# One segment's attention by halves of queries, masked keys by DMA, and a re-valued order

## The chip, the cores and the metric

The kernel runs on one core of one Trainium2 chip. The time is the device time of one execution in microseconds (us). A profiled execution gives a span (first to last instruction) and, beside it, its own device time, which is a little longer.

## What is computed

Two layers of the same pair of blocks run over a sequence of 2048 rows of 512 features: memory-augmented attention (32 heads of 16 features, four segments of 512 rows), then a gated feed-forward part of width 1792. The essential lines:

```python
# attention, per segment s of 512 rows; M and z carry over from segment to segment
logits = einsum('bhqd,bhkd->bhqk', qs, ks) * scale + mask     # causal inside the segment
a_dot = einsum('bhqk,bhkd->bhqd', softmax(logits), vs)
a_mem = einsum('bhld,bhde->bhle', phi(qs), M) / (einsum('bhld,bhd->bhl', phi(qs), z) + 1e-6)
o = g * a_mem + (1 - g) * a_dot
M, z = M + phi(ks)^T vs, z + sum(phi(ks))
# network, twice over
x = x + attention(layernorm(x));   x = x + (gelu(n @ w_gate) * (n @ w_up)) @ w_down   with n = layernorm(x)
```

Segment 0 has no memory, so its attention is the causal part alone. All inputs and the output are bf16.

## The kernel before

**Numbering.** `k` counts segments over both layers, 0 to 7; `Att(k)` and `Ffn(k)` (L610, L1019) are the attention and the feed-forward part of one of them. Attention of segment k+4 needs the output of `Ffn(k)`, and attention of k needs the memory of k-1. So the feed-forward work of one segment can stand beside the attention of the next.

**An order written ahead of time.** No loop nest runs on the chip. The function `order` (L286) holds a small simulation with one clock per engine (`Clocks`, `Engine`), a list of pieces of TensorE work (`Item`) and lists of jobs for VectorE, ScalarE, GpSimd and the SP queue. It walks forward in planned time, picks the next piece by due times and slacks, and emits the instruction there and then. Each engine's instructions are thus a fixed sequence, and semaphores make one wait for another. The due times come from the table `POLICY` of some 45 values: `gate_step`, `early`, `hold`, `cap` and so on. A change of any value may reorder the whole program, on each engine. Jobs carry a slack: `URGENT`, `SOON` or `NORMAL`, smaller first. When TensorE has nothing ready, it runs a filler product on the tile `warm`.

**Attention in rounds.** A segment's scores are 36 rounds (`STEPS`), nine for each block `b` of 128 columns (eight heads: four of parity 0, four of parity 1). A round is 256 columns of scores for four heads, in four row tiles of TensorE (L939). Rounds are issued in pairs into PSUM; ScalarE takes each pair in two exponentials of 128x1024 (L1399) into two of the ten slots of `pt`. The triangles are cut by GpSimd (L1346, L1351) or VectorE (L1356). A block's nine rounds are four of parity 0 (`FULL`), one shared by both parities (`PAIRED`, the diagonal pieces), and four of parity 1. The odd heads need a copy of k with the even heads' rows set to zero, and the shared round one that mixes the two: the masked k, `kx`, made by two instructions per block on VectorE, GpSimd (L417) or ScalarE (L422), whichever the planner picks. `kx` of segments 1 and up alternates between two buffers.

**From scores to the output of a block.** `flush_item` (L943) multiplies the exponentials with v (four column tiles, 40 products) into one PSUM bank for a block and a parity. VectorE turns it (`byq`, L972), inverts the sums (L976), scales (L980) and turns back (`aT`, L987). `flush_item` frees the slots of `pt` that it has used. After all four blocks, `wo` (four tiles of 128 rows, 4 products each) gives the attention output.

**From there to the feed-forward part.** The `wo` tile is added to x (L1028). VectorE takes the row's moments (`bn_stats` L514, `bn_aggr` L522). When all four tiles are in, GpSimd computes the inverse root for the four at once (L527, L532); VectorE scales four tiles (`xn`, L544), TensorE turns them (L586; for the keys in `BY_PE`, else a DMA transpose on SP does it), with `FILL` = 2 filler products on `warm` ahead of each (L584), and they are copied out into `xnT`. Then come 14 gate tiles, 14 up tiles (4 products each) and 4 down tiles of 14 products. The gate waits for all of `xnT`, and in segment 0 also for the memory update, since the gate's buffer `gel_sb` holds v of segment 0 until then.

**SP's queue.** SP issues the weights, the DMA transposes and the shared v (`vz`, L701) in one sequence. The pieces of `w_down` go out at fixed planned times from 94 us on, since q, k and `kx` of segment 0 lie in their place.

Of the kernel before, what the change touches and what calls it, by code (L numbers as in the profile page):

```python
# [12 lines left out]
ALU = mybir.AluOpType  # L13
# [18 lines left out]
VALUES = TPS * VW + 16  # L32
SCALE = DH ** -0.5
# [11 lines left out]
PAIRED = [(ki, P * ki, C, C * ki) for ki in range(TPS)]  # L45


def round_of(t):

    b, i = divmod(t, ROUNDS)  # L50
    if i == SHARED:
        return b, (0, 1), PAIRED, None
    par = int(i > SHARED)
    return b, (par,), FULL[i - par * (SHARED + 1)], DIAG[i - par * (SHARED + 1)]


BY_PE = {("xnTf", 0), ("xnTf", 1), ("xnTf", NK - 1)}
BANKS = 8
# [3 lines left out]
URGENT, SOON, NORMAL = -4.0, -1.5, 0.0  # L62
XN_BUFS = 4
BUFS = 6
FILL = 2
# [4 lines left out]
    flush_wait=60.178, piece_slack=2.474, kb_slack=40.846, mem_slack=-55.59, margin=2.052, qk_due=-2.997, e_q=-1.628,  # L70
    e_k=2.444, exp_slack=-52.211, e_slack=213.844, phi_slack=26.757, gelu_slack=17.711, act_evict=-7.207,
    first_evict=15.014, gate_step=70.271, up_due=-0.803, up_step=0.121, down_due=2.855, down_step=15.464,
    upd_due=-0.036, kb_act=30.625, vz_slack=-37.946, x_dve=-2.928, v0_due=-11.201, x1_at=-44.439, x2_at=17.127,
    x3_at=25.097, x3_load=11.502, direct=4, gelu_tiles=7, look=4.219, lag=0.576, wv_at=-5.253, xn_pool=39.635,
    kb_pool=0.131, cut_pool=-3.745, at_pool=5.073, pe_turns=0, gate_due=2.262, shun=0.829, col_gap=3.113, hold=3,
    early=122.612, starve=0.322, near=-0.26, cap=2, soon=21.81, columns=0)
# [15 lines left out]
class Engine:  # L92
# [24 lines left out]
    def serve(self, now):  # L117
# [9 lines left out]
        job = min((j for j in jobs if j[0] + self.LATENCY <= start + 0.03), key=lambda j: j[0] + j[1] + (  # L127
# [123 lines left out]
class Item:  # L251


    def __init__(self, due, ready, ops, done, kind, ps, after="start"):
        self.after = after
        self.due = due if callable(due) else lambda: due
        self.ready, self.ops, self.done, self.kind, self.ps = ready, ops, done, kind, ps
        self.posted = 0.0
# [27 lines left out]
def order(pol, nc, cst, seg, wrk, psp, A_x, A_wq, A_wk, A_wv, A_wo, A_beta, B_x, B_w_gate, B_w_up, B_w_down, out):  # L286
# [87 lines left out]
    nc.vector.reduce_sum(out=masks[:, 1:2], in_=bd[:, 16:P:32], axis=mybir.AxisListType.X)  # L374

    tmp_e2 = cst.tile([P, H], F32, name="tmp_e2")
# [34 lines left out]
    def masked_copies(ready, slack, kx, kf, told):  # L411
# [4 lines left out]
        def vector(which, eng):  # L416
            return lambda: eng.tensor_scalar(out=kx[:, :, C * which:C * which + P], in0=kf, scalar1=masks[:, which:which + 1],  # L417
                                             scalar2=None, op0=ALU.mult)
# [6 lines left out]
        ck.dve.post(ready, slack, (Port(0.35), vector(0, nc.vector), None),  # L425
                    (Port(0.35), vector(1, nc.vector), told), taken=taken)
        ck.pool.post(ready, slack + pol.kb_pool, (Port(1.57, True), vector(0, nc.gpsimd), None),
# [50 lines left out]
    def soon(name, n=KT, part=1.0):  # L478

        t = ck.pe - 0.1 - ck.back  # L480
# [20 lines left out]
    class Norm:  # L501
        def __init__(self, key, tt0, tag, slack, free):
            self.key, self.tt0, self.tag, self.slack, self.free = key, tt0, tag, slack, free
            self.mv, self.n, self.left = None, 0, TPS
# [3 lines left out]

        def stats(self, j, ready):
            def emit():  # L510
                if self.mv is None:
                    self.mv = self.small("mv", 2)
# [3 lines left out]
            def told(t):  # L516
                self.n += 1
                if self.n == TPS:
                    self.scales(t)

            ck.dve.post(ready, self.slack, (0.66, emit, None),
                        (0.17, lambda: nc.vector.bn_aggr(out=self.mv[:, j, :], in_=self.st6[:]), told))  # L522

        def scales(self, ready):
            def first():
                self.ve = wrk.tile([P, TPS, 1], F32, tag="lnve", name="ve")
                nc.gpsimd.tensor_scalar(out=self.ve[:], in0=self.mv[:, :, 1:2], scalar1=EPS_LN, scalar2=None,  # L527
                                        op0=ALU.add)

            def second():  # L530
                self.rs = self.small("rs", 1)
                nc.gpsimd.tensor_tensor(out=self.rs[:], in0=self.ve[:], in1=mhalf[:], op=ALU.pow)  # L532

            ck.pool.post(ready, URGENT, (0.25, first, None),
                         (1.05, second, lambda t: ck.when(self.free, lambda: self.start(max(t, ck.pe)))))

        def start(self, ready):
            self.xnT = seg.tile([P, KT, L], BF16, tag=self.tag, bufs=1, name="xnT")
            for j in range(TPS):
                xn_slots.take(lambda n, j=j: bufs.take(lambda i: self.row(j, n, i, max(ready, ck.pe))))  # L540

        def normed(self, j, i, eng=nc.vector):
            xn = buffer(i, "xn")
            eng.tensor_scalar(out=xn[:], in0=x_sb[:, self.tt0 + j, :], scalar1=self.mv[:, j, 0:1],  # L544
# [3 lines left out]
        def row(self, j, n, i, ready):  # L548
# [13 lines left out]
            def told(t):  # L562
                if self.by_pe():
                    items.append(self.turn_item(j, xn, t, landed))
                else:
                    turn_later(t, self.slack, lambda: self.xnT[:, :, j * P:(j + 1) * P], lambda: xn()[:], landed,
                           pol.margin)

            on_dve_or_pool(ready, self.slack, pol.xn_pool if self.key[0] == "xnTa" else None, Port(0.405),
# [958 lines left out]
```

## Time and profile before

| | |
|---|---|
| time, median of 3 runs | 542.61 us (542.56 to 542.7) |
| profiled execution, its own time | 543.32 us |
| its span | 541.6 us |
| TensorE busy | 522.7 us (97%) |
| VectorE busy | 439.1 us (81%) |
| ScalarE busy | 434.3 us (80%) |
| GpSimd busy | 297.4 us (55%) |

A line of the page's groups reads: source line, engine, operation, output tile, input tiles, shapes, count, then busy us, mean ns of one, and the idle time of the engine ahead of it. A row of the view by stretches gives the stretch, its length, the busy time and the count of each engine in the order TensorE, weight loads, VectorE, ScalarE, GpSimd, then TensorE's granted clock, the DMA share and GB/s. A row of the timeline gives start, length, engine, line, operation, tiles, shapes and count, and in brackets the idle time ahead of it. TensorE counts as busy during filler products too.

### The profile page before, as it was taken

How to read it: one execution, taken by the hardware profiler on the slowest of the kernel's cores; microseconds unless marked ns; L12 is line 12 of the kernel's file. 1: busy time of each engine (PE TensorE's matmuls, PEld its weight loads, DVE VectorE, ACT ScalarE, POOL GpSimd, SP SyncE). 2: the span in 40 equal slices, each digit the busy share in tenths (PEclk: the TensorE clock that was granted, in tenths of full speed). 3: DMA queues.
4: the chain of work that ended last, by engine and by line, in shares of the span. 5: the costliest groups of instructions: out<-in, count | busy, mean ns of one | idle time of the engine just before them, and what ended most of it. 6: DMA issues, size and time to landing. Idle time of an engine off the chain costs nothing.

```text
span 541.6 us, 22747 instructions
## 1 busy us (share of the span) xinstructions
PE 522.7 (97%) x10016; PEld 274.0 (51%) x10075; DVE 439.1 (81%) x814; ACT 434.3 (80%) x533; POOL 297.4 (55%) x346
## 2 busy tenths in 40 slices
PE   8899999999999999999999999999999999999997
PEld 4454555454554445554555545554465456555444
DVE  7899998899988998679987699879778786786342
ACT  5999899997998987999899899997887978910320
POOL 4887589487857986155871595716863164300000
PEclk9999999999999999999999999999999999999999
DMA  8477410620240124101332211411313014000001
GB/s 270 63 123 178 136 41 7 153 52 14 33 79 14 24 41 89 33 2 32 42 70 32 34 34 20 72 22 33 61 33 40 15 13 81 4 3 27 14 0 40
DMA packets 69141, 28.08 MB, mean 52 GB/s; under 512 B 53426, under 2 KB 69042, under 8 KB 69042
## 3 DMA queue, kind: packets, MB, share of 16 engines
q1 hardware_dynamic: 68752, 26.36, 24.5%
q8 instruction: 79, 1.29, 1.0%
q10 hardware_dynamic: 290, 0.26, 0.1%
q14 instruction: 20, 0.16, 0.1%
HBM read 9.70 MB, written 2.10 MB: 22 GB/s over the span
## 4 chain that ended last, share of the span: by engine, by line
PE 88%; DVE 6%; issue 2%; ACT 1%; DMA 1%; POOL 0%; ACTq 0%; DVEq 0%; POOLq 0%
PE ps L476 39%; PE ps L471 34%; PE ps L939 8%; PE ps L955 7%; ACT pt L1399 1%; DVE xn L544 1%; DMA xnT<-xn 1%; DVE st L514 1%; DVE x_sb L1028 1%; DMA x_sb<-in_A_x_dram 1%; PE ps L866 1%; DVE kx L417 0%; DVE st L1184 0%; DVE pt L1356 0%; DVE byq L972 0%
## 5 line engine op out<-in xcount | busy, mean ns | idle before, releaser
L1399 ACT ACTIVATE pt<-ps 128x1024 bf16<-128x1024 f32 x288 | 278.9, 1030 | 38.4 <-PE ps L939 34.1
L1346 POOL TENSOR_SCALAR_AFFINE_SELECT pt<-pt 128x256 bf16<-128x256 bf16 (+1 forms) x192 | 109.6, 584 | 132.5 <-ACT pt L1399 129.0
L1093 DVE TENSOR_TENSOR gel_sb<-gel_sb,ps 128x512 bf16<-128x512 bf16 x112 | 75.3, 683 | 33.8 <-PE ps L476 20.5
L1028 DVE TENSOR_TENSOR x_sb<-x_sb,ps 128x512 bf16<-128x512 bf16 (+1 forms) x68 | 43.1, 643 | 26.9 <-PE ps L476 16.4
L764 POOL TENSOR_SCALAR e<-e 128x512 bf16<-128x512 bf16 x39 | 61.4, 1577 | 4.6 <-ACT e L741 3.6
L476 PE MATMUL ps<-wd_sb,gel_sb 128*128 128x512 bf16 (+1 forms) x287 | 58.7, 351 | 1.5 <-issue 1.3
L972 DVE STREAM_TRANSPOSE byq<-ps 128x512 f32<-128x512 f32 x64 | 45.1, 706 | 16.1 <-PE ps L955 15.6
L471 PE MATMUL ps<-xnT,wg_sb 128*32 128x512 bf16 x916 | 56.1, 380 | 0.1
L476 PE MATMUL ps<-xnT,wu_sb 128*128 128x512 bf16 x213 | 51.1, 379 | 1.5 <-issue 1.1
L476 PE MATMUL ps<-xnT,wg_sb 128*128 128x512 bf16 x207 | 49.9, 379 | 1.6 <-issue 1.4
L471 PE MATMUL ps<-xnT,wu_sb 128*32 128x512 bf16 x888 | 51.0, 379 | 0.0
L471 PE MATMUL ps<-wd_sb,gel_sb 128*32 128x512 bf16 (+1 forms) x816 | 45.3, 361 | 0.0
L476 PEld LDWEIGHTS <-gel_sb 128*128 128x128 bf16 x300 | 27.9, 98 | 25.3 <-issue 0.4
L514 DVE BATCH_NORM_STATS2 st<-x_sb 128x6 f32<-128x512 bf16 x60 | 40.4, 673 | 0.2
L1351 POOL TENSOR_SCALAR_AFFINE_SELECT pt<-pt 64x1024 bf16<-64x1024 bf16 x26 | 32.4, 1247 | 9.8 <-ACT pt L1399 9.0
L955 PE MATMUL ps<-pt,vaug 128*32 128x256 bf16 (+2 forms) x1344 | 35.2, 238 | 1.5 <-issue 1.0
L471 PEld LDWEIGHTS <-wu_sb 128*32 128x32 bf16 x888 | 23.0, 97 | 22.3 <-issue 0.9
L955 PEld LDWEIGHTS <-vaug 128*32 128x32 bf16 x1344 | 27.6, 97 | 12.6 <-issue 4.1
L476 PEld LDWEIGHTS <-wu_sb 128*128 128x128 bf16 x226 | 20.8, 98 | 24.8 <-issue 1.2
L471 PEld LDWEIGHTS <-wg_sb 128*32 128x32 bf16 x916 | 23.4, 97 | 19.1 <-issue 1.3
L1152 ACT ACTIVATE gel_sb<-gel_sb 128x3584 bf16<-128x3584 bf16 (+1 forms) x14 | 32.4, 2351 | 0.0
L939 PE MATMUL ps<-q,kx 32*128 32x64 bf16 (+2 forms) x1120 | 31.2, 217 | 0.7 <-ACT pt L1399 0.5
(145 smaller groups left out, 892.7 us busy)
## 6 DMA issues: line engine op xcount, KB each, us to landing
vz<-vaug SPq DMA_DIRECT2D x14, 136.0 KB, 3.0
wg_sb<-in_B_w_gate_dram SPq DMA_DIRECT2D x8, 224.0 KB, 3.6
wu_sb<-in_B_w_up_dram SPq DMA_DIRECT2D x8, 224.0 KB, 2.9
wd_sb<-in_B_w_down_dram SPq DMA_DIRECT2D x7, 256.0 KB, 4.4
x_sb<-in_A_x_dram SPq DMA_DIRECT2D x3, 512.0 KB, 6.5
out_dram<-x_sb SPq DMA_DIRECT2D x12, 128.0 KB, 1.7
xnT<-xn SPq DMA_TRANSPOSE x48, 2.9
wk_sb<-in_A_wk_dram SPq DMA_DIRECT2D x2, 256.0 KB, 4.7
```

Source lines behind the costliest of these rows:

```text
L471: nc.tensor.matmul(out[r], lhsT=lhsT[:, r], rhs=rhs, start=start, stop=stop, tile_position=(0, 32 * c))
L476: nc.tensor.matmul(out, lhsT=lhsT, rhs=rhs, start=start, stop=stop)
L514: nc.vector.bn_stats(out=self.st6[:, 0, :], in_=x_sb[:, self.tt0 + j, :])
L764: lambda eng: eng.tensor_scalar(out=e[0][:], in0=e[0][:], scalar1=1.0, scalar2=None, op0=ALU.min), summed)
L939: nc.tensor.matmul(ps_all[:, bank, o + c0:o + c0 + n], lhsT=lhsT, rhs=self.q[rows, b, q0:q0 + n], start=True, stop=True, tile_position=(32 ...
L955: nc.tensor.matmul(ps()[32 * j:32 * j + 32, q0:q0 + n], lhsT=va[:, ki * VW + g:ki * VW + g + 32], rhs=pt_all[:, places[i], j, c0:c0 + n], ...
L972: nc.vector.transpose(out=self.byq[:, par, :, :].rearrange("p a c -> p (a c)"), in_=ps()[:])
L1028: ck.dve.post(ck.made(), slack, (0.15 + 0.00104 * (c1 - c0), lambda: nc.vector.tensor_tensor(out=xt, in0=xt, in1=ps()[:, 0:c1 - c0], op=AL ...
L1093: ck.dve.post(ck.made(), NORMAL, (0.683, lambda: nc.vector.tensor_tensor(out=g, in0=g, in1=ps()[:], op=ALU.mult), lambda t: (ps.read(t), e ...
L1152: return (0.205 + 0.427 * (f1 - f0), lambda: nc.scalar.activation(out=g, in_=g, func=ACT.Gelu_apprx_tanh), lambda t: self.gelu_done(t, f0, ...
L1346: nc.gpsimd.affine_select(out=view, in_=view, pattern=[[0, 4], [0, n], [1, C]], compare_op=ALU.is_ge, fill=0.0, base=C, channel_multiplier=-1)
L1399: nc.scalar.activation(out=pt_all[:, s0:s0 + 2, 2 * p:2 * p + 2, :].rearrange("p r h c -> p h r c"), in_=ps_all[:, pair[0]:pair[1] + 1, :] ...
```

## The change

Five things change together.

1. Segment 0 (`HALVED`) gets another table of rounds. Block 0 stays whole. Blocks 1 to 3 are done by halves of the 512 queries: first the early half of blocks 1, 2 and 3, then the late half of 3, 1 and 2. A flush now covers both parities and 256 queries, in one PSUM bank. The count of rounds (36) and of products stays. `wo` tile j waits only for the half of queries that it needs.
2. `Norm` of segment 0's feed-forward part takes its tiles in pairs: moments, inverse root and scaling of tiles 0 and 1 no longer wait for tiles 2 and 3. Tile 2 (`QUICK`) gets its mean from the sum that the addition to x now delivers, and its variance from a square on ScalarE. Jobs of this path have the new slack `CHAIN` (-60), and the picker of jobs may choose one of them that becomes ready up to 0.25 us (else 0.03 us) later than the engine is free: the look-ahead.
3. `kx` of segments 1 to 3 (`SENT`) is filled by eight DMAs on SP each, 16 rows at a time, after all four blocks of k are there; the rest of both buffers is zeroed once by GpSimd at the start. The first of the two instructions of the other segments' copies covers 64 columns in place of 128 per tile.
4. `FILL` is 0. Gate tiles 5 to 13 of segment 0 (`HELD` = 5) no longer wait for the memory update and stand first.
5. All values of `POLICY` but a few are new; `pe_turns` goes from 0 to 1, so that `xnT` of attention segment 1 is turned by TensorE.

```diff
+HELD = -(-VALUES // L)
+HALVED = (0,)
+SENT = (1, 2, 3)
+EARLY = [(1, 192, 64, 0), (0, 64, 192, 64)]
+LATE = [([(3, 448, 64, 0), (2, 320, 192, 64)], 2), ([(0, 256, 256, 0)], 0), ([(1, 256, 256, 0)], 0)]
...
+    if halved:
+        a1, s12, a2 = add(early(1)), add([(shared((1, 0), (1, 1), (2, 0), (2, 1)), None)]), add(early(2))
+        a3, s3 = add(early(3)), add([(shared(*((3, ki) for ki in range(TPS))), None)])
+        units += [(1, 0, [(BOTH, [*a1, *s12])]), (2, 0, [(BOTH, [*a2, *s12])]), (3, 0, [(BOTH, [*a3, *s3])])]
+        units.append((3, 1, [(BOTH, [*s3, *add(late(3))])]))
+        l1 = add(late(1))
+        s12 = add([(shared((1, 2), (1, 3), (2, 2), (2, 3)), None)])
+        units += [(1, 1, [(BOTH, [*l1, *s12])]), (2, 1, [(BOTH, [*s12, *add(late(2))])])]
...
+QUICK = {("xnTf", k): (2,) for k in HALVED}
...
-URGENT, SOON, NORMAL = -4.0, -1.5, 0.0
+CHAIN, URGENT, SOON, NORMAL = -60.0, -4.0, -1.5, 0.0
-FILL = 2
+FILL = 0
...
-    early=122.612, starve=0.322, near=-0.26, cap=2, soon=21.81, columns=0)
+    x3_load=4.232, direct=4, gelu_tiles=5, look=3.52, lag=0.617, wv_at=-19.153, xn_pool=81.09, kb_pool=-7.488,
+    cut_pool=32.248, at_pool=5.776, pe_turns=1, gate_due=0.712, shun=0.703, col_gap=5.799, hold=8, early=11.714,
+    starve=0.314, near=-51.121, cap=5, soon=53.674, columns=0, kd_slack=156.304)
...
-        job = min((j for j in jobs if j[0] + self.LATENCY <= start + 0.03), key=lambda j: j[0] + j[1] + (
+        job = min((j for j in jobs if j[0] + self.LATENCY <= start + (0.25 if j[1] <= CHAIN else 0.03)), key=lambda j: j[0] + j[1] + (
...
+    nc.gpsimd.memset(kxs[1], 0.0)
...
-            return lambda: eng.tensor_scalar(out=kx[:, :, C * which:C * which + P], in0=kf, scalar1=masks[:, which:which + 1],
-                                             scalar2=None, op0=ALU.mult)
+            n = P if which else C
+            return lambda: eng.tensor_scalar(out=kx[:, :, C * which:C * which + n], in0=kf[:, :, 0:n],
+                                             scalar1=masks[:, which:which + 1], scalar2=None, op0=ALU.mult)
...
+                nc.vector.scalar_tensor_tensor(out=xt, in0=ps()[:], scalar=1.0, in1=xt, op0=ALU.mult, op1=ALU.add,
+                                               accum_out=made[0][:])
...
+                nc.scalar.activation(out=junk[:], in_=xt, func=ACT.Square, scale=float(D) ** -0.5, bias=self.mv[:, j, 0:1],
+                                     accum_out=self.mv[:, j, 2:3])
...
+                nc.gpsimd.tensor_tensor(out=self.rs[:, j0:j0 + n, :], in0=self.ve[:], in1=mhalf[:, 0:n, :], op=ALU.pow)
...
+                for r, odd in list(parts):
+                    c, n = (C, P) if odd else (0, C)
+                    ck.sp.post(ck.pe, pol.kd_slack, (0.62, lambda r=r, c=c, n=n: nc.sync.dma_start(
+                        out=kx[r:r + 16, :, c:c + n], in_=kf[r:r + 16, :, 0:n]), told))
...
-                return Item(k + 0.61 + 0.001 * j, lambda: soon(("aT", k)),
-                            dense(ps, pairs), done, kind="wo", ps=ps, after=("aT", k, 3))
+                return Item(k + 0.61 + 0.001 * j, lambda: soon(("aTh", k, j // 2), eager=k in HALVED),
+                            dense(ps, pairs), done, kind="wo", ps=ps, after=("aTh", k, j // 2, 3))
...
-                            lambda: ck.has(("xnTf", k)) and (("down", k - 1) if k else ("upd", 0)) in ev,
+                            lambda: ck.has(("xnTf", k)) and (k == 0 and ft >= HELD or (("down", k - 1) if k else ("upd", 0)) in ev),
...
+    nc.gpsimd.memset(kxs[0], 0.0)
```

More of the change, by code (lines that the diff above doesn't have):

```diff
@@ L1 @@
 import heapq
-from collections import defaultdict
 from contextlib import ExitStack
@@ L528, in first @@
                                         op0=ALU.add)
             def second():
[L531 to L539, printed above, removed]
+                if self.rs is None:
+                    self.rs = self.small("rs", 1)
```

292 lines of the change are left out of this document (197 added, 95 removed).

## The prediction

> **What bounds the kernel now.** I read the page's busy times first, then TensorE by stretches of 20 us, then the filler products by the same stretches, then the timeline where the two show a hole. The page's row of busy times:
>
> ```profile
> PE 522.7 (97%) x10016; PEld 274.0 (51%) x10075; DVE 439.1 (81%) x814; ACT 434.3 (80%) x533; POOL 297.4 (55%) x346
> ```
>
> TensorE is the bound by its share, but the share counts fillers and hides holes. Stretches (TensorE, weight loads, VectorE, ScalarE, GpSimd):
>
> ```profile
> 20.00:40.00 20.00, 18.28 (x427) 10.04 (x432) 18.61 (x44) 19.47 (x28) 16.84 (x19) 1.00 0.72 117
> 60.00:80.00 20.00, 18.61 (x462) 10.89 (x467) 19.06 (x40) 18.40 (x25) 15.42 (x18) 1.00 0.29 72
> 80.00:100.00 20.00, 19.79 (x340) 10.40 (x336) 17.05 (x27) 19.77 (x24) 14.88 (x15) 1.00 0.17 38
> 120.00:140.00 20.00, 18.35 (x481) 10.53 (x477) 19.57 (x40) 16.87 (x22) 16.18 (x21) 1.00 0.08 17
> 140.00:480.00 340.00, 333.08 (x6923) 173.88 (x6952) 284.68 (x512) 297.91 (x352) 192.60 (x222) 1.00 0.22 38
> ```
>
> The same view for the tile `warm` alone (TensorE, weight loads, VectorE):
>
> ```profile
> 20.00:40.00 20.00, 1.71 (x30) 1.03 (x30) 0.00 (x0) 1.00 0.72 117
> 60.00:80.00 20.00, 2.59 (x54) 1.72 (x54) 0.00 (x0) 1.00 0.29 72
> 120.00:140.00 20.00, 1.88 (x29) 1.22 (x29) 0.00 (x0) 1.00 0.08 17
> 480.00:500.00 20.00, 0.83 (x8) 0.57 (x8) 0.00 (x0) 1.00 0.05 15
> ```
>
> Idle plus filler is what TensorE does not give to the result: 1.72 + 1.71 = 3.43 us in 20 to 40, 1.39 + 2.59 = 3.98 in 60 to 80, 1.65 + 1.88 = 3.53 in 120 to 140, against 0.21 in 80 to 100, which has no filler. From 140 to 480 it is 340 - 333.08 = 6.92, or 0.41 per 20 us. So three early holes together hold 10.9 us, and most of what an edit can win lies there. The hole in 60 to 80 is the path from segment 0's last block to its feed-forward part:
>
> ```profile
> 61.58 0.29 PE L955 MATMUL ps<-pt,vz 128*32 128x64 bf16 x16
> 64.73 1.46 PE L476 MATMUL ps<-wo_sb,aT 128*128 128x512 bf16 x6
> 71.79 0.51 PE L471 MATMUL ps<-warm 128*32 128x128 bf16 x24
> 76.49 0.38 PE L586 MATMUL ps<-ident,xn 128*128 128x128 bf16 x4
> 78.80 2.63 PE L471 MATMUL ps<-xnT,wg_sb 128*32 128x512 bf16 x44
> ```
>
> ```profile
> 61.99 0.72 DVE L972 STREAM_TRANSPOSE byq<-ps 128x512 f32<-128x512 f32 x1
> 62.74 0.35 DVE L976 RECIPROCAL r<-byq 128x32 f32<-128x32 f32 x1
> 63.13 0.69 DVE L980 TENSOR_TENSOR ab<-byq,r 128x512 bf16<-128x512 f32 x1
> 63.85 0.71 DVE L987 STREAM_TRANSPOSE aT<-ab 128x512 bf16<-128x512 bf16 x1
> 69.32 1.26 DVE L1028 TENSOR_TENSOR x_sb<-x_sb,ps 128x512 bf16<-128x512 bf16 x2
> 71.32 0.66 DVE L514 BATCH_NORM_STATS2 st<-x_sb 128x6 f32<-128x512 bf16 x1
> 72.02 0.18 DVE L522 BATCH_NORM_AGGREGATE mv<-st 128x2 f32<-128x6 f32 x1
> 72.29 0.23 POOL L527 TENSOR_SCALAR ve<-mv 128x4 f32<-128x4 f32 x1 [0.31 <-DVE mv L522]
> 72.60 1.04 POOL L532 TENSOR_TENSOR rs<-ve,mhalf 128x4 f32<-128x4 f32 x1
> 73.91 1.85 DVE L544 TENSOR_SCALAR xn<-x_sb,mv,rs 128x512 bf16<-128x512 bf16 x4
> 77.55 1.20 ACT L462 ACTIVATE xnT<-ps 128x512 bf16<-128x512 bf16 x2
> ```
>
> From the end of the last product with v (61.87) to the first gate (78.80) it takes 16.93 us. TensorE has other work (v, `wo`, segment 1's scores) until the first filler at 71.79, and from there 7 us with little to do.
>
> **The change, part by part. Halves, pairs and the square (edits 1, 2).** Work on TensorE stays: per block 20 pieces of four products before, 4 for an early and 6 for a late half over both parities after, again 20. The new path behind the last late half, from the rows: turn 0.72, then half of 0.35, 0.69 and 0.71 plus some fixed part, 1.1 together; `wo` tiles 2 and 3, eight products by 1.46/6, 1.9; addition, moments of tile 3 0.63 + 0.66 + 0.18 = 1.47 (tile 2's square runs beside them on ScalarE); GpSimd 1.27; two `xn` 0.92; one turn 0.38; copy out 0.60; and six hand-overs of about 0.12 (61.87 to 61.99), 0.7. That is 9.1 us instead of 16.9: the gates could start at 71.0, ahead of the first filler at 71.79, and the hole of 3.98 would close to the level of a stretch without fillers, a gain of 3.8. But VectorE is busy 19.06 of 20 there with jobs of about 0.7 us, and whoever comes finds one running: six entries of the path into VectorE (turn, addition, moments, the two `xn`, the turn back) at some 0.3 each are an estimated 1.8 us. With these the gates start at 72.8, and 1.0 of the hole stays. I take -2.8; ends -3.8 and 0. On VectorE a half flush adds three fixed costs for each of three blocks; by the shortest row of a small operation (0.18) 9 x 0.18 = 1.6 us, hidden by the removal below, 0 to +0.5 if not. What is late next: the `w_down` pieces, whose planned times do not move.
>
> ```profile
> 100.96 2.38 SPq L305 DMA_DIRECT2D wd_sb<-in_B_w_down_dram  x3
> wd_sb<-in_B_w_down_dram SPq DMA_DIRECT2D x7, 256.0 KB, 4.4
> L471 PE MATMUL ps<-wd_sb,gel_sb x40: 379/379/380, 111.7 to 114.9; 128*32 128x512 bf16 x40
> ```
>
> The last lands at about 103.3 + 4.4 = 107.7, the first down product runs at 111.7: 4 us of lead, which a shift of 3 to 4 does not use up, but a larger one would. So this caps the gain near 4 to 6 rather than costing anything.
>
> **Masked k by DMA (edit 3).** Until 140 us the copies for segments 1 to 3 are these:
>
> ```profile
> L422 ACT ACTIVATE kx<-kf,masks x10: 508/618/737, 34.6 to 118.7; 128x256 bf16<-128x256 bf16 x5, 128x512 bf16<-128x512 bf16 x5
> L417 DVE TENSOR_SCALAR kx<-kf,masks x10: 342/600/820, 35.2 to 116.8; 128x512 bf16<-128x512 bf16 x10
> L939 PE MATMUL ps<-q,kx x240: 184/198/279, 66.1 to 138.3; 32*128 32x64 bf16 x74, 32*128 32x256 bf16 x24, 32*128 32x192 bf16 x22
> vz<-vaug SPq DMA_DIRECT2D x14, 136.0 KB, 3.0
> L701 SPq DMA_DIRECT2D vz<-vaug x14: 590/599/1262, 62.0 to 418.6; - x14
> ```
>
> Some 6 us each leave ScalarE (10 x 0.62) and VectorE (10 x 0.60); GpSimd made the rest, and loses them too. ScalarE paces the scores of segments 0 and 1 (19.47 and 19.77 of 20). It is this relief that lets segment 1's scores keep up when the feed-forward work ahead of them starts sooner; without it the hole of 120 to 140 would grow by what the hole of 60 to 80 loses. I count it as holding that hole at 3.53, so 0; ends -3.3 (the hole closes) and +3.7 (all of edits 1 and 5 is given back). Price of the DMAs: 24 issues of 0.6 on SP, 14.4 us of a queue that stands still most of the time; one lands 3.0 us after issue (row of `vz`, 256 runs each as here), so a set of eight takes 7 x 0.6 + 3.0 = 7.2 us. Segment 1's copies are made from 34.6 to about 38 and first read at 66.1, so 28 us of cover; those of 2 and 3 have more. Behind the eight in SP's queue wait weights and turned tiles; with 28 us of cover the planner can put the eight after them. 0. The Trainium skill ("DMA: Bandwidth & Descriptors", Specifications) speaks against it: under 512 B a transfer makes the engine read, modify and write, and its runs here are 128 or 256 B. By that, at twice 3.0 us each and one after another, the eight would take 48 us, segment 1 would wait 20 us, and the sum would be +16. The same page (Why small descriptors are slow) limits the penalty to HBM. No run shown has transfers of such short runs; the row of `vz`, whose two halves go out 0.6 us apart and land 3.0 us after their issue, bears out overlap, and the sum goes by it.
>
> Zeroing the buffers on GpSimd is new, and the first fill stands ahead of the first inverse root:
>
> ```profile
> 0.82 0.20 POOL L356 MEMSET ident<- 128x128 bf16 x1
> 2.32 0.15 POOL L368 MEMSET tri<- 128x64 bf16 x1
> 5.58 0.71 POOL L1194 TENSOR_TENSOR rs<-mv,mhalf 128x2 f32<-128x2 f32 x1 [2.52 <-DVE mv L1190]
> ```
>
> 64 columns more cost 0.05, so 3072 columns cost an estimated 2.5 us, in an idle time of 2.52. I take +0.1; ends 0 and +0.5. The second fill stands behind the last of these roots, ahead of no work that TensorE waits for.
>
> **Fillers (4) and the turn of segment 1 (5).** The eight fillers in 480 to 500 stand in a stretch where TensorE is full: they cost at most their 0.83 and, since they overlap the products behind, I take -0.3. Those of the early holes are inside the holes. In 20 to 40 the one long named wait is for the DMA transposes of segment 1:
>
> ```profile
> PE ps L471 <- DMA xnT<-xn: 0.8, 1, 0.8
> ```
>
> Turning by TensorE removes it, and some fillers with it: -0.9; ends 0 and -3.2.
>
> **The other values of the policy.** They reorder everything from 140 on, in a way that the trace of before can't show. The nearest rows are the shortfall of 0.41 per 20 us there and 0.21 in the best early stretch: equal to that it would win 340/20 x 0.20 = 3.4, and as far to the other side it would lose 3.4. I take 0.
>
> Sum: -2.8 + 0.1 - 0.3 - 0.9 + 0 + 0 = -3.9. Against the profiled execution's own 543.32 that is 539.4; the median of the runs shown is 0.7 lower, so 538.7.
>
> **The rivals.** (a) More: the relief of ScalarE also closes much of the hole at 120 to 140, or the order after 140 is tighter. VectorE at 19.57 of 20 in that stretch speaks against the first. -3.9 - 3.0 gives 535.7, and with both 534. (b) No change: segment 1's score stream does not come sooner, the feed-forward work of segment 0 runs out earlier, and the hole at 120 to 140 grows by 3.7: 542.4. For it speaks ScalarE's 19.77 in 80 to 100, against it the 6 us taken from it. (c) Slower, by the slots of `pt`:
>
> ```profile
> L1399 ACT ACTIVATE pt<-ps 128x1024 bf16<-128x1024 f32 x288 | 278.9, 1030 | 38.4 <-PE ps L939 34.1
> L1351 POOL TENSOR_SCALAR_AFFINE_SELECT pt<-pt 64x1024 bf16<-64x1024 bf16 x26 | 32.4, 1247 | 9.8 <-ACT pt L1399 9.0
> ```
>
> Before, a flush used five rounds of the ten slots. A late half uses six and the shared one: seven, and three are left, one pair. That pair keeps ScalarE busy for 2 x 1.03 = 2.1 us, while the mask of the shared round on GpSimd (2 x 1.25) and the flush (0.7) take 3.2 us. ScalarE stands 1.1 us at each of two late halves, and as much longer as TensorE puts the flush off behind other pieces. The path to the gates starts that much later. From 3.9 us of standing in all it decides: at 3 us a late half it is 6, and 544.8. Against it: VectorE can cut the mask, and a policy value makes the plan take such flushes at once. (d) The new order after 140 costs its 3.4 and the early win is small: 543.9 at a win of 2. (e) The change of `kx` doesn't do what it says: the DMAs come late behind weights and segment 1 stands. It needs 28 - 7.2 = 21 us of delay beyond the landing; each us more costs one, so 545 and up.
>
> **How the numbers follow.** Forecast 0.50 (536.5 to 541.4); (a) 0.13; (b) 0.10; (c) 0.18; (d) 0.05; (e) 0.04. A change of 0.2% (1.1 us) is about what this kernel's measurement can tell. Faster: 0.50 + 0.13 = 0.63; within: 0.10; slower: 0.27. The range leaves out the lower end of (a) and the upper ends of (c) and (e): 534.5 to 545.
>
> **What would show it.** In the changed trace the first gate of segment 0 stands 6 us or less behind the last `wo` product's addition and about 11 us behind the last product with v; fillers plus idle in 60 to 80 fall from 3.98 to about 1.2, and those in 120 to 140 stay near 3.5; no `kx` instruction is on an engine before 140; no product on `kx` waits for a DMA; GpSimd's first inverse root starts by 5.7. The prediction is wrong if the gap behind the exponentials of blocks 3 and 1 exceeds 2 us, if the hole returns at 120 to 140, if the first down product waits for `w_down`, or if the shortfall from 140 to 480 leaves 6.9 by more than 2.

## The result, and the profile after

The changed kernel takes 549.59 us, median of four runs (548.74 to 550.44), against 542.6 for the kernel before: 1.0129 times the time, 95% interval 1.0111 to 1.0146. I had predicted 538.7, with 545.0 as the upper end. The profiled execution's own time is 550.44 us, its span 548.7.

The page's row of busy times, and then the view by stretches of the changed kernel (same columns as before):

```profile
PE 533.1 (97%) x9951; PEld 273.5 (50%) x9951; DVE 437.3 (80%) x827; ACT 431.0 (79%) x527; POOL 275.0 (50%) x333
```

```profile
0.00:20.00 20.00, 15.79 (x110) 7.70 (x111) 14.47 (x39) 10.42 (x19) 13.59 (x24) 0.91 0.61 184
20.00:40.00 20.00, 19.97 (x414) 10.27 (x416) 18.43 (x42) 19.41 (x29) 17.65 (x20) 1.00 0.29 54
...
60.00:80.00 20.00, 17.53 (x284) 8.19 (x281) 13.91 (x33) 14.89 (x21) 6.91 (x10) 0.91 0.69 145
...
120.00:140.00 20.00, 17.34 (x453) 9.76 (x441) 17.70 (x34) 16.14 (x18) 15.82 (x19) 0.91 0.31 50
...
140.00:480.00 340.00, 338.49 (x7015) 175.00 (x7017) 289.99 (x530) 300.14 (x355) 188.58 (x228) 1.00 0.23 38
```

The same view for the tile `warm` alone:

```profile
20.00:40.00 20.00, 0.28 (x2) 0.15 (x2) 0.00 (x0) 1.00 0.29 54
...
60.00:80.00 20.00, 0.30 (x5) 0.36 (x6) 0.00 (x0) 0.91 0.69 145
...
120.00:140.00 20.00, 2.07 (x25) 1.24 (x25) 0.00 (x0) 0.91 0.31 50
```

The row of 0 to 20 in the kernel before:

```profile
0.00:20.00 20.00, 17.37 (x136) 8.21 (x139) 15.06 (x42) 14.26 (x25) 12.29 (x24) 1.00 0.61 187
```

The hole of 20 to 40 is gone: idle plus filler is 0.03 + 0.28 = 0.31 where it was 3.43. That of 60 to 80 is smaller, 2.47 + 0.30 = 2.77 where it was 3.98. But 0 to 20 now stands idle for 4.21 us in place of 2.63, and 120 to 140 loses 2.66 + 2.07 = 4.73 where it was 3.53. The column after GpSimd's is the granted clock: it is 1.00 in all stretches of the profile before, and 0.91 in three here. Narrower stretches show what that is, three windows at half:

```profile
10.10:13.30 3.20, 3.13 (x19) 2.50 (x20) 1.18 (x4) 0.73 (x2) 0.00 (x0) 0.50 1.02 333
74.90:78.20 3.30, 3.30 (x34) 1.16 (x27) 2.32 (x8) 2.68 (x4) 0.05 (x1) 0.50 0.60 153
136.40:139.60 3.20, 2.85 (x18) 1.07 (x18) 2.41 (x6) 3.05 (x4) 2.58 (x5) 0.50 0.02 6
```

The first loss is at the very start. The timeline of the changed kernel (GpSimd, VectorE, TensorE):

```profile
3.12 2.66 POOL L419 MEMSET kx<- 128x3072 bf16 x1
5.88 1.52 POOL L1348 TENSOR_TENSOR rs<-mv,mhalf 128x2 f32<-128x2 f32 x2
7.22 2.75 POOL L1368 MEMSET kx<- 128x3072 bf16 x1
...
4.91 0.88 DVE L1344 TENSOR_SCALAR mv<-mv 128x2 f32<-128x2 f32 x1
...
6.63 0.73 DVE L640 TENSOR_SCALAR xn<-x_sb,mv,rs 128x512 bf16<-128x512 bf16 x2 [0.31 <-POOL rs L1348]
...
7.44 3.00 DVE L640 TENSOR_SCALAR xn<-x_sb,mv,rs 128x512 bf16<-128x512 bf16 x2
...
10.17 1.03 PE L692 MATMUL ps<-ident,xn 128*128 128x128 bf16 x8 [2.24 <-DVE xn L640]
```

The same two steps in the kernel before:

```profile
7.43 0.74 DVE L544 TENSOR_SCALAR xn<-x_sb,mv,rs 128x512 bf16<-128x512 bf16 x2 [0.21 <-POOL rs L1194]
...
7.90 0.72 PE L596 MATMUL ps<-ident,xn 128*128 128x128 bf16 x8 [0.17 <-DVE xn L544]
```

The second zero fill runs from 7.22 to 9.97, and VectorE's scaling of tiles 2 and 3, started at 7.44, takes 3.00 us in place of 0.74. TensorE stands 2.24 us, then gets half its clock for 3.4 us, and the first exponential ends at 15.7 us in place of 12.0. The first fill does the same on a small scale: VectorE's step on the moments (`mv`, L1344) beside it takes 0.88 us in place of 0.17 and ends at 5.79, as the fill ends at 5.78.

The second loss is on the way into segment 0's feed-forward part, the third at `w_down`. The waits of TensorE in the changed kernel (us in total, times, longest):

```profile
PE ps L692 <- DVE xn L640: 2.9, 2, 2.2
PE ps L985 <- DMA phik<-e: 2.2, 2, 1.2
...
PE ps L524 <- DMA wd_sb<-in_B_w_down_dram: 1.2, 1, 1.2
```

Both DMA waits come from SP's queue. Its timeline in the changed kernel:

```profile
66.04 1.24 SPq L770 DMA_DIRECT2D kx<-kf  x2
...
67.97 1.97 SPq L770 DMA_DIRECT2D kx<-kf  x2
70.04 2.55 SPq L490 DMA_TRANSPOSE phik<-e  x2
...
98.10 3.27 SPq L352 DMA_DIRECT2D wd_sb<-in_B_w_down_dram  x5
109.39 1.19 SPq L490 DMA_TRANSPOSE phik<-e  x1
110.63 0.57 SPq L352 DMA_DIRECT2D wd_sb<-in_B_w_down_dram  x1
111.29 1.19 SPq L490 DMA_TRANSPOSE phik<-e  x1
112.53 0.57 SPq L352 DMA_DIRECT2D wd_sb<-in_B_w_down_dram  x1
```

VectorE and the gates, in the same kernel's timeline:

```profile
65.26 0.08 DVE L864 DVE_READ_ACCUMULATOR e<-wd_sb,e 128x1 f32 x1
...
74.64 0.29 DVE L1013 COPY macc<-ps 128x128 f32<-128x128 f32 x1 [1.59 <-PE ps L985]
...
76.38 0.73 DVE L640 TENSOR_SCALAR xn<-x_sb,mv,rs 128x512 bf16<-128x512 bf16 x2
...
80.96 1.05 PE L524 MATMUL ps<-xnT,wg_sb 128*32 128x512 bf16 x16
```

The last `e` is done at 65.34, but its transpose goes out only at 70.04, behind `w_up` and six of the eight DMAs of segment 2's masked k. These could go later: in the runs below that issue them from 66 or 70 us on, no product waits for them. TensorE waits for it, VectorE's copy of the memory sum (`macc`) waits 1.59 us for TensorE, and `xn` of the new path stands behind that copy in VectorE's queue. The first gate runs at 80.96, later than before (78.80). At 110 the same thing: the last two pieces of `w_down`, out by 103.3 before, stand behind one transpose each and go out at 110.63 and 112.53. The first down product runs at 111.39; a later one waits 1.2 us for a piece.

### The profile page after: what moved, and what is told of

Same layout as the page of the kernel before. It is cut to its first block, busy times and chain, and to the rows that moved or that the text cites. A ratio compares the mean times of both kernels' runs of the same rounds, so it can differ in the third digit from the quotient of the medians.

```text
span 548.7 us, 22580 instructions
## 1 busy us (share of the span) xinstructions
PE 533.1 (97%) x9951; PEld 273.5 (50%) x9951; DVE 437.3 (80%) x827; ACT 431.0 (79%) x527; POOL 275.0 (50%) x333
## 4 chain that ended last, share of the span: by engine, by line
PE 72%; DVE 0%; issue 0%
PE ps L529 33%; PE ps L524 27%; PE ps L1056 6%; PE ps L1085 5%; PE ps L985 0%; PE ps L682 0%; DVE x_sb L1176 0%
## 5 line engine op out<-in xcount | busy, mean ns | idle before, releaser
L529 PE MATMUL ps<-xnT,wu_sb 128*128 128x512 bf16 x265 | 61.3, 380 | 0.0
L524 PE MATMUL ps<-wd_sb,gel_sb 128*32 128x512 bf16 (+1 forms) x972 | 54.1, 364 | 2.2 <-DMA wd_sb<-in_B_w_down_dram 1.2
L529 PE MATMUL ps<-wd_sb,gel_sb 128*128 128x512 bf16 (+1 forms) x261 | 51.5, 348 | 0.0
L883 POOL TENSOR_SCALAR e<-e 128x512 bf16<-128x512 bf16 x32 | 48.7, 1527 | 4.9 <-ACT e L860 4.0
L524 PE MATMUL ps<-xnT,wu_sb 128*32 128x512 bf16 x732 | 42.7, 379 | 0.0
L529 PEld LDWEIGHTS <-wu_sb 128*128 128x128 bf16 x265 | 24.6, 98 | 29.2 <-issue 0.6
L514 DVE CAST gel_sb<-ps 128x512 bf16<-128x512 f32 x40 | 27.2, 685 | 11.5 <-PE ps L524 8.6
L524 PEld LDWEIGHTS <-gel_sb 128*32 128x32 bf16 x972 | 24.5, 97 | 21.4 <-issue 3.7
L529 PEld LDWEIGHTS <-wg_sb 128*128 128x128 bf16 x227 | 21.1, 98 | 24.8 <-issue 0.6
L1306 ACT ACTIVATE gel_sb<-gel_sb 128x2560 bf16<-128x2560 bf16 (+2 forms) x15 | 32.5, 2207 | 0.0
```

What stands on the lines that cost most here:

```text
L524: nc.tensor.matmul(out[r], lhsT=lhsT[:, r], rhs=rhs, start=start, stop=stop, tile_position=(0, 32 * c))
L529: nc.tensor.matmul(out, lhsT=lhsT, rhs=rhs, start=start, stop=stop)
L883: lambda eng: eng.tensor_scalar(out=e[0][:], in0=e[0][:], scalar1=1.0, scalar2=None, op0=ALU.min), summed)
```

## The experiments

Theory: the time is lost to three delays beside the main idea, namely the zero fills (they hold VectorE), the masked-k DMAs of segment 2 in SP's queue, and the last `w_down` pieces. Rivals: the order from 140 us on (policy), the new path itself, or the half clock alone. "n-th exponential" is the end of the n-th instruction on `pt` on ScalarE, a mark of how far the work has come; the order is kept in all runs of one kernel, so there the same n is the same work.

**The fills in the kernel before.**

```diff
+    nc.gpsimd.memset(kxs[1], 0.0)
     masks = cst.tile([P, 2], F32, name="masks")
...
     first_scale(2, 4)
+    nc.gpsimd.memset(kxs[0], 0.0)
```

> The kernel before with nothing added but the two fills of kx with zeros on GpSimd, at the two places where the changed kernel has them; the values are overwritten later, so the result is the same. Theory A: the start alone costs 3.7 us (first exponential at 15.7 in place of 12.0, a half clock in the first 15 us), and most of it stays to the end: 546. Rival: the kernel before has holes at 20 to 40, 70 to 80 and 130 to 140, which take a late start up: 543 to 544.

547.49 us (546.88 to 547.99), 1.0076 times the kernel before (1.0053 to 1.0099). The row of `xn` in its timeline:

```profile
7.64 3.04 DVE L545 TENSOR_SCALAR xn<-x_sb,mv,rs 128x512 bf16<-128x512 bf16 x2 [0.21 <-POOL rs L1195]
```

Nothing of the change but two fills, and most of the loss is there: 4.9 us by the medians, 4.1 by the ratio, more than theory A had (546). Part of it is clock here too, half from 8.3 to 15.1 us.

**The fills later, and half as long.** First both fills at planned 22 and 40 us, then only the second half of the second one at 40.

```diff
-    nc.gpsimd.memset(kxs[1], 0.0)
...
-    nc.gpsimd.memset(kxs[0], 0.0)
...
+    ck.at(22.0, lambda: nc.gpsimd.memset(kxs[1], 0.0))
+    ck.at(40.0, lambda: nc.gpsimd.memset(kxs[0], 0.0))
```

> The changed kernel (549.6 us) with its two fills of kx with zeros moved out of the start, to planned times 22 and 40 us on GpSimd; every engine's order is otherwise the same. Theory A (the loss is made of local delays that add up): the two xn of tiles 2 and 3 take 0.75 us again in place of 3.00, TensorE does not wait 2.24 us for them, the clock stays at 1.00 up to 20 us, the first exponential ends near 12.0 in place of 15.7, and all later work comes 3.5 us sooner: 546.1. Theory B (the new order is worse in itself, and early delays vanish in its holes at 70 to 80 and 120 to 150): the start gains 3.5, but the end stays at 549 or above.

547.36 us (546.19 to 550.44), 1.0096 (1.0063 to 1.0129). The first exponential is back at 11.8, but against the same order without fills on GpSimd (the first run of the ladder below) the 22nd ends 1.2 us late and the 25th 5.1: the fill at 40 fell on `xn` of segment 1, and the clock is at half from 47.1 to 50.5. Of the 7.0 us 2.2 came back, where theory A had 3.5; the rest of the fills' price is paid at another place.

```diff
-    nc.gpsimd.memset(kxs[0], 0.0)
+    nc.gpsimd.memset(kxs[0][:, 0:2], 0.0)
+    late_zero = [lambda: nc.gpsimd.memset(kxs[0][:, 2:4], 0.0)]
...
+    ck.at(40.0, late_zero[0])
```

> The changed kernel with half of the second fill (1536 columns) at the start and the other half at a planned 40 us. If VectorE's xn of tiles 2 and 3 stand for as long as GpSimd's fill lasts, the fill takes 1.4 us, the two xn end near 9.0 in place of 10.4, TensorE stands about 0.9 us in place of 2.24, and the first exponential ends near 14.0 at full clock, or 15 if the clock is halved all the same. If the stand has another cause than the fill's length, the two xn end at 10.4 as before.

One execution, 545.51 us; its trace is what counts here.

```profile
7.23 1.47 POOL L1368 MEMSET kx<- 128x1536 bf16 x1
...
7.45 1.71 DVE L640 TENSOR_SCALAR xn<-x_sb,mv,rs 128x512 bf16<-128x512 bf16 x2
```

The half fill takes 1.47 us, the pair of `xn` beside it 1.71 us (3.00 beside a whole fill of 2.75, 0.74 beside none). TensorE stands 0.96 us in place of 2.24, there is no half clock, and the first exponential ends at 13.0. So VectorE stands for as long as the fill lasts.

**A busy TensorE at the start.** Nine filler products of 512 columns ahead of the turns of tiles 2 and 3 (`first_turn(2)`), fills left where they are.

```diff
+    keep_warm(9, BANKS - 2)
     n0.first_turn(2)
```

> The changed kernel, with the fills of zeros where they are, and nine filler products of 512 columns between the turns of tiles 1 and 2, where TensorE stands for 2.24 us. If the half clock from 10.0 to 13.4 comes from TensorE standing there, it stays at 1.00 and the products behind run at full speed: the first exponential ends 1.3 us sooner (14.4 in place of 15.7), and the time is 548.2. If the half clock has another cause, nothing changes: 549.6. If the fillers run at half clock themselves, 551.

547.67 us (547.15 to 549.94), 1.0101 (1.0077 to 1.0125). The clock is 1.00 there and the first exponential ends at 14.3 in place of 15.7. Without the fills it ends at 11.7 in the same order, so 1.4 of the 4.0 us go with the half clock and the rest with the stand. So the clock alone isn't the cause.

**Segment 2's masked k behind segment 1's v.**

```diff
-                    ck.sp.post(ck.pe, pol.kd_slack, (0.62, lambda r=r, c=c, n=n: nc.sync.dma_start(
-                        out=kx[r:r + 16, :, c:c + n], in_=kf[r:r + 16, :, 0:n]), told))
+                    def go(r=r, c=c, n=n):
+                        nc.sync.dma_start(out=kx[r:r + 16, :, c:c + n], in_=kf[r:r + 16, :, 0:n])
+
+                    ck.sp.post(ck.pe, pol.kd_slack, (0.62, (lambda go=go: ck.at(67.5, go)) if k == 2 else go, told))
```

> The changed kernel with the eight small DMAs of segment 2's kx issued behind the shared v of segment 1 in place of ahead of phik; all else in the same order. Theory A: SP reaches the last two phik transposes some 4 us sooner, TensorE's two waits for them (2.2 us) and the half clock from 74.8 to 78.3 go, the first gate comes 3 us sooner (80.96 to about 78), and the time is 546.4. Theory B: the gates come sooner, but the hole at 130 to 150 takes it up: 549.

547.66 us (546.65 to 550.72), 1.0102 (1.007 to 1.0134). From the 37th to the 41st exponential it takes 6.8 us in place of 9.7, so the jump at 65 to 77 us is gone. The time lies between the two theories; alone this is worth 1.9 us, less than the fills.

**Both: fills late, segment 2's DMAs late.**

> Both edits of the two runs before together. Theory A: the two gains add, 549.6 - 3.5 - 3.2 = 542.9, level with the kernel before. Theory B: 547 to 549. If the gains are one and the same (the first shifts the second away): 546.

547.85 us (545.26 to 548.91), 1.0103 (1.0078 to 1.0127), no better than either, as theory B had it. The timeline of its fastest execution shows why the gains do not add:

```profile
39.63 4.44 DVE L639 TENSOR_SCALAR xn<-x_sb,mv,rs 128x512 bf16<-128x512 bf16 x3
...
39.95 2.65 POOL L1406 MEMSET kx<- 128x3072 bf16 x1
```

The late fill holds VectorE again. Moving a fill about on GpSimd can't answer the question here; it has to leave the engine.

**The ladder.** The three causes are taken away one after the other. First the zeroing: two DMAs from the zero columns of `vz`, behind the load of x in SP's queue.

```diff
-    nc.gpsimd.memset(kxs[1], 0.0)
...
-    nc.gpsimd.memset(kxs[0], 0.0)
...
+        for i in (1, 0):
+            load(kxs[i].rearrange("p b t c -> p (b t c)").rearrange("p (r c) -> p r c", r=2),
+                 vz[:, 0:1536].unsqueeze(1).to_broadcast([P, 2, 1536]))
```

> The changed kernel with one difference: the two buffers of masked k are zeroed by two DMAs from SP's queue in place of two fills on GpSimd; the order of all else is kept. Theory (the fills cost what they cost in the kernel before, 547.49 - 542.6 = 4.9): xn of tiles 2 and 3 back to about 0.8 us, first exponential at 11.8 in place of 15.7, no half clock before 60, and a time of 549.6 - 4.9 = 544.7. Rival (the late start only hides the later wait at the turn into segment 0's feed-forward part, which then grows by as much): first exponential at 11.8 too, but 548 or more.

544.87 us (543.45 to 546.6), 1.0038 (1.0023 to 1.0053): 4.7 us below the changed kernel, as the theory had it. The pair of `xn` is back to its old length, and the first exponential ends at 11.7:

```profile
7.16 0.74 DVE L639 TENSOR_SCALAR xn<-x_sb,mv,rs 128x512 bf16<-128x512 bf16 x2 [0.21 <-POOL rs L1347]
```

Then segment 2's DMAs behind segment 1's v, as above:

> The run before with one more difference: the eight masked-k DMAs of segment 2 stand behind segment 1's v in SP's queue; the loads of w_down stay where the changed kernel has them. It differs from the version at 542.1 by the w_down loads alone. Theory (three causes that add up: fills, queue, w_down): 1 to 2 us below the run before, the exponentials behind the plan by under 1 at 77 us, and TensorE waits 1 to 1.3 us for w_down at about 112: 543 to 543.5. Rival (w_down is nothing by itself, it was late only because the rest was): no wait for w_down over 0.4 us and 542.1 as with the early loads.

543.62 us (542.07 to 544.7), 1.0013 (1.0000 to 1.0026). The two intervals overlap, so this step of 1.3 is the least sure; in its profile the first gate stands at 73.41 against 74.84. TensorE still waits 1.1 us for `w_down`. Then the last two pieces of `w_down` go out with the fifth:

```diff
-        late_pieces.append((94.0 + 2.0 * h, 256, lambda r=r: load(
-            wd_sb[:, r, :], B_w_down.rearrange("(ft p) n -> p ft n", p=P)[:, r, :])))
+        late_pieces.append((94.0 + 2.0 * h, 256, lambda h=h: [load(
+            wd_sb[:, r, :], B_w_down.rearrange("(ft p) n -> p ft n", p=P)[:, r, :])
+            for r in [slice(2 * i, 2 * i + 2) for i in ((h,) if h < 4 else (4, 5, 6) if h == 4 else ())]]))
```

> The changed kernel, all engines' orders kept, with three edits on SP and GpSimd: kx is zeroed by two DMAs from the zeros in vz behind the last load of x, in place of two fills on GpSimd; segment 2's eight kx DMAs go behind the shared v of segment 1; the last two pieces of w_down are issued with the fifth. Theory A (local delays of SP's queue and of VectorE beside GpSimd's fill): exponentials 21 to 25 lose the 2.3 to 4 us that the late fill cost in the first and third run, the wait of 1.2 us for w_down goes, no half clock appears, and the time is 3 us under the best of the third run's (545.3): 541 to 542.5, level with the kernel before or 0.2% under it. Theory B (the order itself is no better on the chip): 545 or more although these waits are gone. If the DMAs of zeros delay x or wv at the start, the first products with v stand for up to 4 us.

542.1 us (540.22 to 542.68), 0.9976 times the kernel before (0.9963 to 0.9989). By these intervals it is faster than both kernels. Its stretches, then those of `warm`, and its first gate:

```profile
20.00:40.00 20.00, 19.96 (x426) 10.12 (x415) 18.59 (x44) 19.40 (x28) 17.08 (x18) 1.00 0.37 82
...
60.00:80.00 20.00, 18.85 (x444) 9.66 (x443) 15.31 (x33) 17.99 (x25) 10.13 (x14) 1.00 0.63 111
...
120.00:140.00 20.00, 17.50 (x417) 9.82 (x416) 16.48 (x34) 18.32 (x22) 17.39 (x21) 0.91 0.27 59
...
140.00:480.00 340.00, 339.77 (x6969) 175.14 (x6970) 288.54 (x526) 298.79 (x352) 181.56 (x221) 1.00 0.22 36
```

```profile
60.00:80.00 20.00, 0.66 (x6) 0.42 (x6) 0.00 (x0) 1.00 0.63 111
...
120.00:140.00 20.00, 3.23 (x39) 1.90 (x40) 0.00 (x0) 0.91 0.27 59
```

```profile
73.81 1.05 PE L524 MATMUL ps<-xnT,wg_sb 128*32 128x512 bf16 x16
```

So the three delays cost 4.7 us (fills), 1.3 (DMAs of segment 2) and 1.5 (`w_down`), 7.5 in all, where the change lost 7.0. What is left of the change is a small gain: 0.5 us by the medians, 0.24% (1.3 us) by the ratio. Five of the 23 runs of the kernel before beside it had a mean clock of 0.997 and averaged 544.7 us; they weigh on the ratio and hardly on the median.

**The clock in the hole of 120 to 140.** With the causes gone, a half clock at 127.9 to 131.3 remains. First the kernel before without its filler products of 128 columns, its order kept:

```diff
-                product(ps()[:, 0:P], warm[:], wide[:, 0, :])
+                if ck.mode == "columns" or ck.mode == "rows" and (any(it.kind == "flush" and it.near() for it in items)):
+                    ck.tiling("columns")
+                    ck.count += 4
+                else:
+                    ck.tiling("whole")
+                    ck.count += 1
```

> The kernel before with the order kept and its filler products of 128 columns (44 places, 110 instructions between 20 and 140 us) left out. If they are what keeps the clock at 1.00 in the holes, half clocks of 3.4 us appear near 22, 73 and 135, each worth up to 1.7 us: 544 to 546. If the holes are too short to matter without them, the clock stays 1.00 and the time is 542.6 or a little less, since fillers cost places too.

543.33 us (542.12 to 544.31), 1.0004 (0.9989 to 1.002): no difference that these runs tell, where the theory had 544 to 546. But the mean clock is 0.993 to 0.997 in all ten runs, and 1.000 in 17 of 23 of the kernel before. The profile has one half clock, where the theory had three and the profile before shows none:

```profile
137.50:140.80 3.30, 3.13 (x39) 1.74 (x43) 3.20 (x8) 2.90 (x5) 3.15 (x4) 0.50 0.00 0
```

Then the version of 542.1 with wider fillers:

```diff
-                product(ps()[:, 0:P], warm[:], wide[:, 0, :])
+                product(ps()[:], warm[:], wide)
```

> The version with all three causes taken away (542.1), its filler products of 512 columns in place of 128, order kept. Theory (the half clock at 127.9 to 131.3 comes from a TensorE that is too little busy in the hole of 120 to 140, with 128 columns in a slot of 216 ns): granted clock 1.00 in the hole, 540.5. Rival (the width is nothing, the hole's bare stands bring the half clock): half clock there again and 542.1; if the wide fillers delay the work behind them, 542.5 or more.

542.7 us (542.09 to 543.32), 0.9998 (0.999 to 1.0006). The row of 120 to 140 over all tiles, and that of `warm`:

```profile
120.00:140.00 20.00, 19.79 (x417) 9.87 (x418) 18.10 (x35) 18.99 (x22) 17.50 (x21) 1.00 0.28 61
```

```profile
120.00:140.00 20.00, 7.03 (x40) 2.45 (x41) 0.00 (x0) 1.00 0.28 61
```

The clock stays at 1.00, as the theory had it, but the time does not fall to its 540.5. With 256 columns:

> The version with all three causes taken away (542.1), its filler products of 256 columns in place of 128, order kept. With 512 columns the clock stayed at 1.00 in all twelve runs and the time was no lower (542.7), the fillers taking 7.03 us of 120 to 140 in place of 3.23. Theory (those two effects cancel, and 256 columns keep the clock at half of the fillers' price): clock 1.00 and 541.3. Rival (256 columns are too few to keep the clock): a half clock near 128 to 131 in most runs and 542.1.

541.94 us (540.72 to 542.48), 0.9981 (0.9971 to 0.9991), the clock at 1.00. This is not told apart from 542.1. It doesn't mean that the half clock is free. Of the twelve runs at 542.1, eight have a mean clock of 0.997, which is one window of 3.41 us at half, and average 542.2; the other four have 0.999 or more and average 541.2. So such a window goes with about 1.0 us. This compares runs and not edits, and where the window lies is known for the profiled run alone. The fillers of 512 columns avoid it and average 542.7, those of 256 columns 541.8: they cost about what they save, or more.

## Why the prediction was wrong

**Zero fills (the step that failed).** "I take +0.1; ends 0 and +0.5. The second fill stands behind the last of these roots, ahead of no work that TensorE waits for." The fill's length was right (2.5 estimated, 2.66 and 2.75 measured), and its own engine was free. I asked only what stands behind it on GpSimd, not what runs beside it on VectorE. The first root starts at 5.88, past the 5.7 that I had set, since the first fill, up to 5.78, holds both GpSimd and VectorE's step ahead of the root. The price was 4.7 us in the changed kernel, nine times the upper end, and 4.9 in the one before (4.1 by the ratio). A page of the Trainium skill that I did not weigh has the rule: "SBUF — State Buffer", Who interferes with whom, says that VectorE and GpSimd share one pair of ports, that a scaling by scalars can take both ports, and that who issues first holds the pair for its whole instruction while the other stands. The trace agrees in size: 2.68 us for the first `xn` issued 0.22 us into the fill, against 0.41 for one without, and half of the fill gave half of the stand.

**Masked k by DMA.** "A queue that stands still most of the time" and "the planner can put the eight after them" were wrong: SP issues with hardly a pause from 60 to 72 us, and the planner put six of segment 2's eight ahead of the transposes. I had named who is queued behind them, but given cover (28 us) to the eight's own readers alone and left the rest to the planner; +1.3 in place of 0. The transfers themselves came out nearly as taken; the changed kernel's row of these issues:

```profile
L770 SPq DMA_DIRECT2D kx<-kf x24: 585/606/1342, 39.8 to 134.4; - x24
...
DMA to landing us min/median/max: 2.0/3.0/5.0
```

0.6 us to issue and 3.0 to land; no product on `kx` waits for one, and until 140 us no engine makes a copy for segments 1 to 3. By the Trainium skill ("DMA: Bandwidth & Descriptors", Why small descriptors are slow) the penalty of short runs is limited to HBM. These runs of 128 and 256 B do not take twice the 3.0 us, but the trace can't show that they cost nothing: those of 64 KB land after 3.4 us, and `vz` with 136 KB after 2.5. Rival (e) named lateness of these DMAs for segment 1; the harm was done to others.

**`w_down`.** "The `w_down` pieces, whose planned times do not move" and "caps the gain near 4 to 6 rather than costing anything" were wrong: the issues did move, from 103.3 to 112.5 at the latest, behind transposes that wait for their data. It cost 1.1 to 1.3 us of a named wait and 1.5 in time. The first down product did not wait, a later one did.

**Halves, pairs and the square.** As far as the runs show, right in mechanism. I had the first gate 10.9 us behind the last v product, at 72.8. In the version without the three delays the gate stands at 73.81, 10.5 us behind the last v product (63.28), where it was 16.93 before, and 5.8 us behind the last `wo` product's addition (68.06), where I had set 6. The hole of 60 to 80 falls from 3.98 to 1.15 + 0.66 = 1.81, 2.2 less, where I took 2.8. In the changed kernel the same path takes from 67.32 to 80.96, 13.6, with the late transposes in it.

**The turn of segment 1.** Right in direction, and mis-sized: 3.43 falls to 0.31, near the end of -3.2, where I took -0.9, and the named wait for the DMA transposes is gone. Whether the turn alone does this was not run. Sixteen more turns on TensorE go against it.

**The hole of 120 to 140.** "I count it as holding that hole at 3.53" was wrong. Even without the delays it grows, from 3.53 to 2.50 + 3.23 = 5.73, by 2.2. This is rival (b), whose 3.7 was the upper end: by its account, work that segment 0's feed-forward part now does sooner is missing later, and ScalarE's relief does not hold it. The size fits; why segment 1's scores don't come sooner was not tried.

**Fillers.** Those in 480 to 500 are gone, and the stretch stays full; a gain of at most 0.8.

**Policy.** The term was 0, and its ends of ±3.4 stood on a false reading. These two rows of TensorE's waits are of the kernel before and of the first rung of the ladder:

```profile
PE ps L476 <- issue: 5.9, 37, 0.2
```

```profile
PE ps L528 <- issue: 4.8, 30, 0.2
```

The last version (339.77 of 340 busy in 140 to 480) has the order of that rung and lacks this row. So the gaps of 0.16 us are mostly products that the record lost, and not stands: before, the page counts 10016 products to 10075 weight loads, and the changed kernel 9951 to 9951. The same holds from trace to trace: the first rung counts 9889 to 9951 and has the row, the last version 9951 to 9951. The kernel before with the two fills, the same order, has a whole record of 10075, and its stretch of 140 to 480 is busy for 337.63 us and not 333.08. The 6.92 of idle that I saw there was largely not there. My last sign of failure, that this figure leaves 6.9 by more than 2, could therefore not decide anything.

**Rival (c)** was not seen: between 20 and 80 us ScalarE's exponentials waited 0.3 us for slots of `pt` in the changed kernel.

Against the profile of before, the version at 542.1 has -3.1 (20 to 40), -2.2 (60 to 80), +0.2 (100 to 120), +2.2 (120 to 140) and -0.9 (480 to 500), that is -3.8 (the holes of before are some tenths too large, by 0.16 us for each lost product in them); 16 more turns give back an estimated 0.9 (a row of eight takes 0.61 us and overlaps what follows), and the half clock 1.0 by the runs above, or 1.7 if all of it is lost. That makes -1.9 to -1.2, and the two profiled executions differ by 542.23 - 543.32 = -1.1. So up to 0.8 us is unexplained, and a policy term of that size is not excluded: 140 to 480 can't be compared, with the record of before incomplete there. The sum of the prediction, -3.9, lacked the turns' price, the half clock and rival (b), even where its three delays are gone. (Rival (c) adds up to 544.7 and (d) to 544.0, 0.1 off what stands there.) The parts of the change that remain, halves against pairs against the order, were not run apart, since each gives another order.

## What to carry to other kernels

An operation on an idle engine is free only if what runs beside it on the other engines is free too: ask of a GpSimd fill what VectorE does in those microseconds, and of a DMA issue who is queued behind it, not only who reads it. Before a row's idle time is taken as something to be won, compare the counts of products and of weight loads in it. A change that looks bad as a whole may hold a small gain; take its side effects away one at a time, in the same order of work, before judging the main idea.

## What the runs showed of the hardware

A GpSimd fill of 3072 bf16 columns stops a bf16 scaling on VectorE for its whole length (2.75 us: 3.00 for the pair; 1.47 us: 1.71). Other work of VectorE is held or not by its kind: the small f32 step on `mv` took 0.88 in place of 0.17, and in the run with both fills late a bf16 copy of 128x128 beside the fill took 1.82 in place of 0.44; but two `bn_stats` beside the first fill took 1.29, as they do without it. In one run `xn` is shown 0.32 us ahead of the fill and stands all the same (3.12 us). There GpSimd had a scaling of its own under way (37.92 to 40.00), and the fill followed at once; starts on GpSimd are rough.

The half clock comes in pieces of 3.41 us and not in every execution of one kernel (mean clocks of 0.997 and 1.000 both stand among the twelve runs with the median of 542.1). In the profile of the run with segment 2's DMAs late it stood at 9.3 to 16.1 and 115.1 to 118.5. By the Trainium skill ("TensorE: Matmul & The Clock Gate", Part 1) the clock is full or half, by a free-running window of 3.413 us, and half comes after an idle window. The lengths agree, but an idle window was not needed here. These rows are the windows ahead of the three half clocks in the changed kernel:

```profile
6.57:9.98 3.41, 0.84 (x9) 0.54 (x9) 3.34 (x4) 1.26 (x4) 3.40 (x3) 1.00 1.10 331
71.43:74.84 3.41, 1.26 (x70) 0.88 (x72) 1.75 (x5) 1.33 (x3) 1.02 (x3) 1.00 0.51 112
132.87:136.28 3.41, 2.13 (x53) 1.50 (x46) 3.31 (x7) 3.41 (x5) 2.21 (x4) 1.00 0.45 99
```

TensorE was busy for 0.84, 1.26 and 2.13 of 3.41 us in them. In the version of 542.1 it was 2.20 ahead of the half clock, while in the run with half a fill a window with 1.95 (68.8 to 72.2) was followed by full clock. So the busy time alone does not settle it, and no run here shows what else does.
